# Reordering the last loads of a reading phase: fourth blocks ahead of the streams, raw rows last with no streams between them

## The chip, the cores and the metric

The kernel runs on one core of one Trainium2 chip. The metric is the device time of one execution in microseconds (us), as the median of several runs. In the profile, PE is TensorE (PEld its weight loads), DVE is VectorE, ACT is ScalarE, and SPq is the sequencer that issues the loads and stores.

## The reference

```python
# x: (1, 384, 384, 384) bfloat16, w1d: (1,) bfloat16
g = jnp.einsum("bhwc->bc", x) / (H * W)      # mean of each channel
s = jax.nn.sigmoid(g * w1d[0])               # k = 1, no padding
return x * s[:, None, None, :]
```

Every element must be summed before the first output can be written. x is 113.25 MB and does not fit on the chip, so part of it has to be read a second time.

## The kernel before

A "row" below is one 128 x 384 slab: one position of the arena in each partition, 128 x 384 x 2 = 98,304 bytes. There are 1152. In the **summing phase** each row is loaded and added up by a matmul with ones. Rows end in one of three ways:

- **streams** (785 rows) are summed and then overwritten; the scaling phase reads them again;
- **groups** (296 rows; a "half group" is what one pass of the loop below loads and folds) stay on the chip, packed: a "fold" on VectorE and ScalarE hides the bits of every fourth block in exponent bits of three others that are known to be constant (tested, with a slow way out), so that four rows need the room of three;
- **raw** rows (71) stay as they are, in the space that is free last: 39 rows in three small slots S1, S2, S3, and the scratch areas V, U, Y, T of the folds.

In the **scaling phase** the kept rows are multiplied by the sigmoid and stored, and the streams come through again. The kernel is written as a list of steps with the rows that each reads and writes; waits follow from that list. All loads and stores are issued in order by one sequencer, so a load that must wait for its buffer holds up all loads after it.

```python
S1, S2, S3 = ([slot] for slot in SLOTS)          # 13 rows each
...
BETWEEN = [
    ([], EARLY),                                  # big streams, up to 48 rows a load
    ([], B3), ([], B4),
    ([], B3), ([], AA),
    ([], halves(areas[4])), ([], S1 + S2 + S3),
    (S1, S2, S3 + S1), (S2, S3, S1 + S2 + S3),    # the last two half groups
]
between = sum(n for b in BETWEEN[1:] for where in b for _, n in where)
at = 0
for g, q in enumerate(QS[:BANKED]):
    for lo in range(0, q, 2 * PIECE):
        n = min(2 * PIECE, q - lo)
        *blocks, last = BETWEEN[at]
        cuts = [n * i // len(blocks) for i in range(len(blocks) + 1)]
        for e, f, where in zip(cuts, cuts[1:], blocks):
            group_load(...)                       # three blocks of a piece
            sum_rows(...)
            stream_all(where)
        beside = (U, V)[at % 2]
        group_load(g, 3 * q + lo, 3 * q + lo + n, beside)   # the fourth blocks
        sum_rows(beside, n)
        for k in of_group(g):
            ...                                   # fold(k, ...)
        ...
        stream_all(last)
        at += 1
...
for a, n in SLOTS + [(V, 8), (U, 8), (Y, 8), (T, 5), (T + 5, 3)]:
    take_raw(a, n)                                # load, sum
```

At the end of the summing phase the small slots are thus used in the order S1, S2, S3 as streams, and at once again S1, S2, S3 for raw rows.

## Time and profile before

| | before |
|---|---|
| median of 3 runs | 723.07 us (722.98 to 723.43) |
| span of the profiled run | 721.2 us |
| moved by DMA | 303.87 MB, mean 421 GB/s |
| VectorE busy | 69% of the span |
| TensorE busy | 30% |
| DMA below 360 GB/s | slices 14 and 15 of 40 (252 to 288 us) and the last |

The lines themselves, and how they are read, are in the prediction below. The main dip lies at the turn from the summing to the scaling phase, and the change touches what comes just ahead of it. DMA engines are sixteen, and every load is shared among all of them: the trace has sixteen completion increments for each load.

### The profile page before, as it was taken

How to read it: one execution, taken by the hardware profiler on the slowest of the kernel's cores; microseconds unless marked ns; L12 is line 12 of the kernel's file. 1: busy time of each engine (PE TensorE's matmuls, PEld its weight loads, DVE VectorE, ACT ScalarE, POOL GpSimd, SP SyncE). 2: the span in 40 equal slices, each digit the busy share in tenths (PEclk: the TensorE clock that was granted, in tenths of full speed). 3: DMA queues.
4: the chain of work that ended last, by engine and by line, in shares of the span. 5: the costliest groups of instructions: out<-in, count | busy, mean ns of one | idle time of the engine just before them, and what ended most of it. 6: DMA issues, size and time to landing. Idle time of an engine off the chain costs nothing.

```text
span 721.2 us, 3243 instructions
## 1 busy us (share of the span) xinstructions
PE 213.6 (30%) x1202; PEld 118.9 (16%) x1202; DVE 496.2 (69%) x469; ACT 115.4 (16%) x92; POOL 0.2 (0%) x4
## 2 busy tenths in 40 slices
PE   4677879889877780000000000000000000000000
PEld 2344445545444340000000000000000000000000
DVE  4600006887996729998999998999979994355330
ACT  3600004665774520000100000000000000000000
POOL 0000000000000000000000000000000000000000
PEclk9899999999999995555555555555555555555555
DMA  9999999999999988999999999999999999999997
GB/s 386 426 429 430 444 414 428 432 431 430 427 428 426 418 342 320 408 424 430 432 430 439 424 436 432 427 446 428 428 433 431 441 431 435 422 439 428 438 436 323
DMA packets 19890, 303.87 MB, mean 421 GB/s; under 512 B 2210, under 2 KB 2210, under 8 KB 6434
## 3 DMA queue, kind: packets, MB, share of 16 engines
q1 hardware_dynamic: 19872, 303.67, 98.7%
q8 instruction: 9, 0.15, 0.1%
q14 instruction: 7, 0.06, 0.0%
q10 hardware_dynamic: 2, 0.00, 0.0%
HBM read 190.41 MB, written 113.25 MB: 421 GB/s over the span
## 4 chain that ended last, share of the span: by engine, by line
DMA 56%; DVE 27%; PE 6%; another core or an unknown queue 4%; ACT 2%; SPq 1%; issue 0%; DVEq 0%
DMA arena<-in_x_dram 41%; DVE arena L433 18%; DMA out_dram<-arena 15%; DVE arena L251 6%; PE bank L227 6%; DVE arena L257 4%; ACT arena L291 2%; SPq L221 1%; ACT s_bf L424 0%; PE bank L505 0%; DVE odd L500 0%; DVE odd_i L509 0%; DVE worst L495 0%; DVEq L112 0%
## 5 line engine op out<-in xcount | busy, mean ns | idle before, releaser
L433 DVE TENSOR_TENSOR arena<-arena,s_bf 128x1536 bf16<-128x1536 bf16 (+8 forms) x102 | 241.8, 2411 | 71.8 <-DMA arena<-in_x_dram 57.5
L251 DVE TENSOR_SCALAR arena<-arena 128x1536 uint16<-128x1536 uint16 (+2 forms) x247 | 145.9, 634 | 111.6 <-DMA arena<-in_x_dram 100.8
L227 PE MATMUL bank<-arena,ones 128*128 128x384 bf16 x1152 | 205.4, 340 | 55.0 <-DMA arena<-in_x_dram 54.9
L227 PEld LDWEIGHTS bank<-arena,ones 128*128 128x128 bf16 x1152 | 114.0, 101 | 146.1 <-DMA arena<-in_x_dram 60.7
L257 DVE TENSOR_TENSOR arena<-arena 128x1536 uint16<-128x1536 uint16 (+2 forms) x114 | 121.0, 1062 | 10.3 <-PE bank L227 8.1
L291 ACT ACTIVATE arena<-arena 128x3072 uint16<-128x3072 uint16 (+1 forms) x38 | 102.5, 2696 | 146.1 <-DVE arena L251 146.1
L361 ACT COPY arena<-bank 128x512 uint32<-128x512 uint32 (+1 forms) x7 | 4.0, 571 | 70.5 <-DMA out_dram<-arena 70.3
L242 PE MATMUL bank<-ones,zeros 128*128 128x384 bf16 x48 | 8.3, 326 | 0.0
L291 ACT ACTIVATION_READ_ACCUMULATOR arena<-arena 128x1 f32 x38 | 7.1, 187 | 0.0
L242 PEld LDWEIGHTS bank<-ones,zeros 128*128 128x128 bf16 x48 | 4.7, 98 | 3.1
L505 PE MATMUL bank<-odd,ones 128*128 128x1 bf16 x1 | 0.2, 187 | 15.8 <-DVE odd L500 15.8
L361 ACT COPY bank<-arena 128x512 uint32<-128x512 uint32 (+1 forms) x7 | 3.6, 567 | 0.0
L505 PEld LDWEIGHTS bank<-odd,ones 128*128 128x128 bf16 x1 | 0.1, 106 | 16.2 <-DVE odd L500 16.2
L424 ACT ACTIVATE s_bf<-bank,w_sc 128x384 bf16<-128x384 f32 x1 | 0.6, 581 | 12.9 <-PE bank L227 12.9
L720 ACT ACT_TABLE_LOAD x1 | 1.3, 1283 | 0.7 <-PEq L736 0.7
L321 DVE TENSOR_SCALAR w_sc<-bank 128x1 f32<-128x1 f32 x1 | 0.2, 157 | 1.1 <-PE bank L316 1.1
L311 DVE MEMSET ones<- 128x128 bf16 x1 | 0.2, 165 | 1.0 <-SPq L106 1.0
L316 PE MATMUL bank<-w_bf,ones 1*128 1x1 bf16 x1 | 0.2, 181 | 2.1 <-DMA w_bf<-in_w1d_dram 2.1
L316 PEld LDWEIGHTS bank<-w_bf,ones 1*128 1x128 bf16 x1 | 0.1, 99 | 2.1 <-DMA w_bf<-in_w1d_dram 2.1
L509 DVE CAST odd_i<-bank 128x1 int32<-128x1 f32 x1 | 0.2, 158 | 0.3 <-PE bank L505 0.3
L495 DVE TENSOR_REDUCE worst<-seen 128x1 f32<-128x38 f32 x1 | 0.2, 182 | 0.0
L500 DVE TENSOR_SCALAR odd<-worst 128x1 bf16<-128x1 f32 x1 | 0.2, 156 | 0.0
(5 smaller groups left out, 0.5 us busy)
## 6 DMA issues: line engine op xcount, KB each, us to landing
arena<-in_x_dram SPq DMA_DIRECT2D x17, 4608.0 KB, 34.5
out_dram<-arena SPq DMA_DIRECT2D x6, 4608.0 KB, 43.9
arena<-in_x_dram SPq DMA_DIRECT2D x21, 1248.0 KB, 11.6
arena<-in_x_dram SPq DMA_DIRECT2D x9, 2304.0 KB, 27.3
out_dram<-arena SPq DMA_DIRECT2D x8, 2304.0 KB, 28.1
arena<-in_x_dram SPq DMA_DIRECT2D x4, 4512.0 KB, 33.6
out_dram<-arena SPq DMA_DIRECT2D x3, 4512.0 KB, 26.7
out_dram<-arena SPq DMA_DIRECT2D x9, 1248.0 KB, 12.0
```

What stands on the lines that cost most here:

```text
L221: lambda: nc.sync.dma_start(out=arena[:, a : a + hi - lo, :], in_=view(xf, r0, n)[:, lo:hi, :]),
L227: return nc.tensor.matmul(acc, lhsT=ones[:], rhs=arena[:, i, :], start=first, stop=last)
L242: lambda: nc.tensor.matmul(acc, lhsT=zeros[:], rhs=ones[:, None, :].to_broadcast([P, C // P, P]), start=False, stop=False),
L251: lambda: nc.vector.tensor_scalar(out=dst, in0=src, scalar1=s0, scalar2=s1, op0=op0, op1=op1),
L257: "DVE", lambda: nc.vector.tensor_tensor(out=dst, in0=a, in1=b, op=op), reads=reads, writes=writes
L291: lambda: nc.scalar.activation(out=y, in_=y, func=ACTF.Copy, accum_out=seen[:, 2 * k + i : 2 * k + i + 1]),
L316: lambda: nc.tensor.matmul(votes, lhsT=ones[0:1, :], rhs=w_bf[0:1, 0:1], start=True, stop=True),
L361: "ACT", lambda: nc.scalar.copy(dst.bitcast(u32), src.bitcast(u32)), reads=reads, writes=writes
L424: lambda: nc.scalar.activation(out=s_bf[:], in_=acc, func=ACTF.Sigmoid, scale=w_sc[:, 0:1]),
L433: lambda: nc.vector.tensor_tensor(out=v, in0=v, in1=s_bf[:, None, :].to_broadcast([P, n, C]), op=Op.mult),
L505: lambda: nc.tensor.matmul(votes, lhsT=ones[:], rhs=odd[:], start=True, stop=True),
L720: nc.scalar.preload_act_table(ACTF.Sigmoid)
```

## The change

The intent: load the fourth blocks of the last two half groups before the streams, so that folds can begin sooner and free the scratch areas; move two 13-row streams out of the small slots to the first stream of the kernel; and load the raw rows last, with nothing streamed between them. The diff, cut to its core (comments mine):

```diff
     BETWEEN = [
...
-        (S1, S2, S3 + S1), (S2, S3, S1 + S2 + S3),
+        (S1, S2 + S3 + S1), (S2, S3 + S1),      # two streams of 13 rows fewer
     ]
...
+            blocks = BETWEEN[at]
+            cuts = [lo + n * i // len(blocks) for i in range(len(blocks) + 1)]
             for e, f, where in zip(cuts, cuts[1:], blocks):
...
+                group_load(g, 3 * e, 3 * f, areas[g][0] + 3 * e)
+                sum_rows(areas[g][0] + 3 * e, 3 * (f - e))
+                if e == lo:                      # fourth blocks with the first part
+                    group_load(g, 3 * q + lo, 3 * q + lo + n, beside)
+                    sum_rows(beside, n)
+                for k in of_group(g):
+                    if e <= pieces[k][1] < f:
+                        fold(k, beside + pieces[k][1] - lo)
+                if g:
+                    stream_all(where)
...
-    for a, n in SLOTS + [(V, 8), (U, 8), (Y, 8), (T, 5), (T + 5, 3)]:
+    for a, n in S2 + V1 + S3 + S1 + [(U, 8), (Y, 8), (T, 5), (T + 5, 3)]:
         take_raw(a, n)
```

The first stream becomes 40 rows instead of 14. The scaling phase has the same order of loads and stores in both kernels.

More of the change, by code (lines that the diff above doesn't have):

```diff
@@ L377, in halves @@
         return [(a, n // 2), (a + n // 2, n - n // 2)]
+    V1 = [(V, 8)]
     EARLY = areas[1:5]
     BETWEEN = [
-        ([], EARLY),
-        ([], B3), ([], B4),
-        ([], B3), ([], AA),
-        ([], halves(areas[4])), ([], S1 + S2 + S3),
-        (S1, S2, S3 + S1), (S2, S3, S1 + S2 + S3),
+        (EARLY,),
+        (B3,), (B4,),
+        (B3,), (AA,),
+        (halves(areas[4]),), (S1 + S2 + S3,),
+        (S1, S2 + S3 + S1), (S2, S3 + S1),
     ]
     between = sum(n for b in BETWEEN[1:] for where in b for _, n in where)
+    first = N_STREAM - between
     at = 0
@@ L391 @@
             n = min(2 * PIECE, q - lo)
-            *blocks, last = BETWEEN[at]
-            cuts = [n * i // len(blocks) for i in range(len(blocks) + 1)]
+            beside = (U, V)[at % 2]
+            blocks = BETWEEN[at]
+            cuts = [lo + n * i // len(blocks) for i in range(len(blocks) + 1)]
             for e, f, where in zip(cuts, cuts[1:], blocks):
-                group_load(g, 3 * (lo + e), 3 * (lo + f), areas[g][0] + 3 * (lo + e))
-                sum_rows(areas[g][0] + 3 * (lo + e), 3 * (f - e))
-                stream_all(where)
-            beside = (U, V)[at % 2]
-            group_load(g, 3 * q + lo, 3 * q + lo + n, beside)
-            sum_rows(beside, n)
-            for k in of_group(g):
-                if lo <= pieces[k][1] < lo + n:
-                    fold(k, beside + pieces[k][1] - lo)
-            if g:
-                stream_all(last)
-            else:
-                first = N_STREAM - between
-                stream_all(EARLY[3:], first % 48)
-                stream_all(EARLY, first - first % 48)
-                folding = True
+                group_load(g, 3 * e, 3 * f, areas[g][0] + 3 * e)
[8 more added lines that the diff above has]
+                    stream_all(where)
+                else:
+                    stream_all(EARLY[3:], first % 48)
+                    stream_all(EARLY, first - first % 48)
+                    folding = True
             at += 1
```

## The prediction

> **What bounds the kernel now.** I read the page first: how full the DMA engines are, slice by slice.
>
> ```profile
> span 721.2 us, 3243 instructions
> ...
> DMA  9999999999999988999999999999999999999997
> GB/s 386 426 429 430 444 414 428 432 431 430 427 428 426 418 342 320 408 424 430 432 430 439 424 436 432 427 446 428 428 433 431 441 431 435 422 439 428 438 436 323
> ```
>
> The busiest compute engine, VectorE, is busy for 69% of the span; the DMA row is at nine tenths or more except in two slices. So the kernel is bound by moving 303.87 MB, and only time in which DMA runs below its usual 430 GB/s can be won. Apart from the first and last slices that is the dip of slices 14 and 15 (counting from 0), 252 to 288 us: the end of the summing phase, in which the rows are read and summed, and the start of the scaling phase. Second view: busy times by window around the dip (columns: window, its length, busy time and count of PE, PEld, DVE, ACT, POOL, granted clock, DMA share, GB/s).
>
> ```profile
> 224.00:248.00 24.00, 18.17 (x106) 9.61 (x104) 19.50 (x28) 12.51 (x9) 0.00 (x0) 1.00 1.01 427
> 248.00:256.00 8.00, 4.90 (x29) 2.38 (x26) 7.54 (x11) 5.81 (x5) 0.00 (x0) 1.00 0.99 380
> 256.00:266.00 10.00, 9.61 (x48) 5.07 (x49) 1.55 (x2) 1.67 (x2) 0.00 (x0) 0.83 1.00 417
> 266.00:276.00 10.00, 4.16 (x24) 2.10 (x24) 4.82 (x4) 0.58 (x1) 0.00 (x0) 0.87 0.40 162
> 276.00:286.00 10.00, 0.00 (x0) 0.00 (x0) 10.00 (x6) 0.00 (x0) 0.00 (x0) 0.50 0.97 408
> 286.00:290.00 4.00, 0.19 (x1) 0.11 (x1) 3.65 (x10) 0.00 (x0) 0.00 (x0) 0.50 1.02 286
> ```
>
> In time lost against 427 GB/s: 248 to 256: 8 x 47/427 = 0.9 us; 256 to 266: 0.2; 266 to 276: 6.2; 276 to 286: 0.4; 286 to 290: 1.3. The large one is the turn from reading to writing. The third view, the chain of waits, says what it is made of (start, length, what):
>
> ```profile
> 254.82 2.87 ACT arena L291 x2
> ...
> 257.70 10.02 DMA arena<-in_x_dram
> 267.71 0.05 issue
> 267.76 2.79 PE bank L227 x16
> 270.55 0.02 issue
> 270.57 0.59 ACT s_bf L424
> 271.16 0.02 issue
> 271.18 14.84 DVE arena L433 x8
> ```
>
> Last raw rows, their matmuls, the sigmoid, the first scaling, the first store: nothing can be written before that, and the change keeps all of it. The chain also puts the last folds (two, 243.05 to 257.70 us) in front of that load, as if they held it up. But the load issued at 257.70 landed 10.0 us later because others stood before it in the queue; the loads of the last raw rows landed one behind the other at the queue's pace. So the folds cost nothing now, and the chain misleads here.
>
> That leaves the 0.9 us of 248 to 256. Fourth view: TensorE in time order, with the idle time before each group in brackets.
>
> ```profile
> 246.04 2.29 PE L227 MATMUL bank<-arena,ones 128*128 128x384 bf16 x13 [1.20 <-DMA arena<-in_x_dram]
> 249.08 2.29 PE L227 MATMUL bank<-arena,ones 128*128 128x384 bf16 x13 [0.75 <-DMA arena<-in_x_dram]
> 252.04 2.29 PE L227 MATMUL bank<-arena,ones 128*128 128x384 bf16 x13 [0.68 <-DMA arena<-in_x_dram]
> 256.32 5.91 PE L227 MATMUL bank<-arena,ones 128*128 128x384 bf16 x25 [2.00 <-DMA arena<-in_x_dram]
> ```
>
> Groups of 13 rows start every 3.0 us, then once after 4.28 us. That late group is the first raw slot, S1. Its load was issued at 248.36, the moment the sums of the streamed rows in the same slot ended (246.04 + 2.29 = 248.33): a wait for the buffer. The view of that one issue says how long it took:
>
> ```profile
> DMA to landing us min/median/max: 7.9/7.9/7.9
> ```
>
> The two raw loads behind it also took 7.9 us, the streamed load before it (issued 243.58) 8.4, so 7.9 us is what a 13-row load takes with almost nothing queued ahead.
>
> **What the Trainium skill says.** "DMA: Bandwidth & Descriptors", section "Anatomy of one DMA", gives 2.0 us plus bytes/436e3 (of a DMA issued by GpSimd): for 13 rows of 98,304 bytes, 4.9 us. The trace has 7.9 us here. The same page, "Why a DMA increments its semaphore by 16 and not by 1", explains the rest: a transfer is complete only when all its engines are. The landing records of the late load agree: its first increment comes 4.9 us after the issue, its last 7.9. I use 7.9. "Perfetto Trace Analysis", "Identifying Performance Opportunities", says that repeating bubbles on the saturated engine can mean too few buffers; here it is one bubble, in a chain of three slots. "TensorE: Matmul & The Clock Gate", Part 1, has the clock halve after about 3.4 us of idling; here 2.0 us came before ten matmuls at about 0.32 us instead of 0.176. They did not set the end: TensorE still waited 0.37 us at 267.76.
>
> **The change, part by part.** The scaling phase keeps its order exactly, so I expect it shifted as a block. In the summing phase:
>
> Moved: two 13-row streams (26 rows) leave the small slots near the end; the first stream, into the large area 4, grows from 14 to 40 rows. Bytes are the same, with two loads fewer. From the landing records a 48-row load needs 0.2267 us a row, a 13-row load 0.229: 26 x 0.0023 = 0.06 us won. Everything between comes 26 x 0.2267 = 5.9 us later. At the start, area 4 now waits for 40 rows to be summed instead of 14; but three 48-row loads (33 us) are queued behind them, and TensorE had summed its first 54 rows by 20.7 us, so nothing runs dry.
>
> Removed: the tight reuse of slots. Before, the end is stream S1, S2, S3, then raw S1, S2, S3: from one use of a slot to the next lie 39 rows, 39 x 0.229 = 8.93 us of DMA. One turn needs a landing (7.86 us in the landing records) plus 13 matmuls (2.29) and handover, some 10.2 us. Short by 1.3 us, once, since all three slots then run equally late. That matches the late landing: 4.28 us after its predecessor instead of 2.97, so 1.31. After, the raw order S2, V, S3, S1 with no streams between gives, from the last stream in the slot: S2: S2, 12 group rows, S3, S1 = 51 rows; S3: S3, S1, raw S2, V's 8 = 47 rows; S1: S1, raw S2, V, S3 = 47. 47 x 0.229 = 10.8 us, 0.5 above the need. The kernel before has one reuse at just 47 rows, the load issued at 243.58, which ran without a bubble. So the 1.3 us go, and nothing takes their place. In bandwidth the same is 0.9 + 0.2 = 1.1 us.
>
> Added: nothing. The folds have the same count and operands; loading the fourth block first lets the first of two folds start 25 rows before the last piece has landed. On my estimate the last fold ends at about 255 instead of 257.7 (the last fourth block lands at 240.2, two folds of 7.3 us each follow), and the last raw loads, for Y and T, are due 10 us after that. This takes nothing from the path, but gives margin.
>
> Sum: 1.1 to 1.3 for the bubble, 0.06 for larger loads, perhaps 0.1 for other reuses that grow (from 51 to 59 rows for the first S1 of group 4). I take 1.3: 723.07 - 1.3 = 721.8.
>
> **Rivals.** First: the folds are on the path, as the chain says, and the end of summing moves with them by 257.7 - 255 = 2.7 us: 720.4. For it speaks the chain; against it that the last loads land at the queue's pace. Second: the 47-row turns are still too short, since raw S3 and S1 follow at that distance twice, with margin 0.5 us, and V's load has no slack either: half the gain is lost, 722.5. The 8.4 us of the load at 243.58 speaks against it. Third: the slow packets at 248 to 256 come from memory or from an instruction fetch (the instruction queue has 9 packets in all, one at 252.6) and not from the waiting slot: no change, 723.0. The wait that ends at the very moment of the issue speaks against it. Fourth: a longer start, with the first wait on area 4 breaking the early stream; a loss of some us, and nothing in the queue's depth points to it.
>
> **Range and chances.** The three runs before lie within 0.45 us. All rivals but the last lie within 720.4 to 723.0; I put 8 in 10 on 720.8 to 722.8. 2% is 14.5 us; the whole dip together is worth 9 us, of which about 6 is untouched, so faster by 2% is all but excluded. Slower by 2% would need a new stall of 14 us, for which I see no place.
>
> **What would show it.** Right: no gap before a 13-row group of matmuls above about 1.3 us from 245 to 265 us; GB/s of 248 to 256 at about 425; the slot waits' loads landing in 8.4 us or more; s_bf written about 1.3 us earlier (269.3 instead of 270.57); the span from there on unchanged, near 450.6 us. Wrong: a new gap before the last raw groups, a TensorE chain starting cold in the last 20 us, or a scaling phase whose length changes by more than 0.3 us although its order is the same.

## The result and the profile after

| | before | after |
|---|---|---|
| median, first comparison | 723.03 us (4 runs) | 722.94 us (4 runs) |
| ratio | | 0.9998, 95% interval 0.9981 to 1.0016 |
| span of the profiled run | 721.2 us | 721.1 us |
| sigmoid starts | 270.57 us | 269.79 us |
| from there to the end | 450.58 us | 451.35 us |

Ratios are the mean time of one kernel's fast runs over that of the other's of the same rounds, so not quite the ratio of the quoted medians. The time is the same within the noise. 722.94 lies outside the predicted range of 720.8 to 722.8, and the predicted 1.3 us were not seen.

The page of the changed kernel, rows as in the prediction:

```profile
span 721.1 us, 3241 instructions
...
DMA  9999999999999978999999999999999999999997
GB/s 377 438 432 426 429 433 428 435 431 425 430 422 429 426 329 333 413 426 427 436 429 439 423 431 436 433 439 426 419 432 433 440 437 427 426 435 437 438 428 321
```

The dip is still where it was. Two instructions fewer: the two loads. The windows around it (columns as in the prediction):

```profile
224.00:248.00 24.00, 18.80 (x109) 9.79 (x106) 21.47 (x29) 16.16 (x13) 0.00 (x0) 1.00 1.01 428
248.00:256.00 8.00, 5.00 (x29) 2.68 (x30) 6.12 (x9) 5.39 (x4) 0.00 (x0) 1.00 1.02 428
256.00:266.00 10.00, 8.12 (x50) 4.50 (x49) 0.00 (x0) 0.00 (x0) 0.00 (x0) 1.00 0.98 410
266.00:276.00 10.00, 3.69 (x22) 1.81 (x20) 5.60 (x5) 0.58 (x1) 0.00 (x0) 0.83 0.40 164
```

The lost bandwidth of 248 to 256 us is back, 428 GB/s instead of 380, just as predicted. Yet the window after it is at 410: some engines are done while others are not (the last load's first increment comes at 265.49 us, its last at 268.78). TensorE in time order shows a late group all the same:

```profile
248.67 2.29 PE L227 MATMUL bank<-arena,ones 128*128 128x384 bf16 x13 [0.82 <-DMA arena<-in_x_dram]
251.65 2.29 PE L227 MATMUL bank<-arena,ones 128*128 128x384 bf16 x13 [0.69 <-DMA arena<-in_x_dram]
255.57 3.59 PE L227 MATMUL bank<-arena,ones 128*128 128x384 bf16 x21 [1.64 <-DMA arena<-in_x_dram]
260.36 2.29 PE L227 MATMUL bank<-arena,ones 128*128 128x384 bf16 x13 [1.21 <-DMA arena<-in_x_dram]
```

The third group starts 3.92 us after the second, where 3.0 is the pace. The load it waits for, raw S2, was issued at 245.29 us, 10.2 us before it was complete. Its issue too waited for the slot (the sums of the streamed rows in S2 ended at 245.26), but two 13-row loads stood ahead of it in the queue. The wait left no gap: the first increments of these loads and of raw S2 (246.13, 249.11, 252.07 us) keep the pace. So the late group has another cause. And the chain of waits near the turn:

```profile
253.43 0.97 DVE arena L257
254.40 0.37 SPq L221
...
254.81 12.12 DMA arena<-in_x_dram
...
266.98 2.79 PE bank L227 x16
269.77 0.02 issue
269.79 0.59 ACT s_bf L425
```

The folds end at 254.4 instead of 257.7 us, and the last load then takes 12.1 us instead of 10.0: it stands in a longer queue, as the prediction said of the misleading chain.

So two questions are open. In the summing phase 1.3 us were expected and 0.78 came. In the scaling phase, whose order is the same, even those were lost again.

### The profile page after: what moved, and what is told of

Its sections match the earlier page's. It is cut to its first block, busy times and chain, and to the rows that moved or that the text cites. A ratio compares the mean times of both kernels' runs of the same rounds, so it can differ in the third digit from the quotient of the medians.

```text
span 721.1 us, 3241 instructions
## 1 busy us (share of the span) xinstructions
PE 212.8 (30%) x1202; PEld 118.5 (16%) x1202; DVE 496.3 (69%) x469; ACT 115.4 (16%) x92; POOL 0.2 (0%) x4
## 4 chain that ended last, share of the span: by engine, by line
DMA 52%; DVE 29%; PE 6%; another core or an unknown queue 4%; ACT 3%; SPq 0%; issue 0%; DVEq 0%
DMA arena<-in_x_dram 37%; DVE arena L434 18%; DMA out_dram<-arena 15%; DVE arena L251 7%; PE bank L227 6%; DVE arena L257 4%; ACT arena L291 3%; SPq L221 0%; ACT s_bf L425 0%; PE bank L506 0%; DVE odd L501 0%; DVE odd_i L510 0%; DVE worst L496 0%; DVEq L112 0%
## 6 DMA issues: line engine op xcount, KB each, us to landing
out_dram<-arena SPq DMA_DIRECT2D x9, 1248.0 KB, 12.1
```

## How the landings are read

The trace records each of the sixteen increments of a load's semaphore, one for each DMA engine. For each load there is therefore a first, a mean and a last landing. ("Leading engine" below is the one that lands first, "last engine" the one that lands last. The increments don't name their engines, so from load to load it need not be the same one. The prof views show only the last increment.) For the last load before the turn (3 rows of T) and, as a starting point, the load with 71 rows still to come, in us:

| kernel | last load: first | mean | last | sigmoid starts | last 71 rows took: first engine | mean | last engine |
|---|---|---|---|---|---|---|---|
| before | 267.39 | 267.95 | 269.54 | 270.57 | 18.24 | 17.46 | 17.55 |
| before_again | 267.46 | 267.98 | 269.18 | 270.11 | 18.05 | 17.36 | 17.04 |
| before_third | 266.98 | 267.55 | 269.23 | 270.26 | 17.81 | 17.10 | 17.48 |
| after | 265.49 | 266.83 | 268.78 | 269.79 | 16.38 | 16.46 | 17.18 |
| after_again | 265.44 | 266.80 | 268.87 | 269.88 | 16.38 | 16.46 | 17.10 |
| after_third | 265.55 | 266.74 | 268.62 | 269.63 | 16.38 | 16.46 | 17.30 |
| v_first | 265.60 | 266.90 | 269.21 | 270.24 | 16.37 | 16.46 | 17.58 |
| fourth_first | 267.47 | 268.22 | 269.67 | 270.70 | 17.43 | 17.42 | 17.23 |
| streams_only | 268.96 | 269.28 | 270.00 | 270.96 | 19.73 | 18.93 | 18.63 |
| fewer_sums | 265.64 | 266.89 | 268.38 | 269.40 | 16.38 | 16.37 | 16.38 |
| s1_at_once | 272.62 | 272.84 | 273.06 | 274.04 | 23.23 | 22.38 | 21.18 |
| no_warm | 265.61 | 266.87 | 268.71 | 269.72 | 16.38 | 16.46 | 17.12 |
| y_split | 265.59 | 266.94 | 269.23 | 270.08 | 16.40 | 16.51 | 17.10 |

"First engine" compares the first landings of the two loads, "last engine" their last landings. The rows are explained one by one below. The first six already say the main thing: the change won 1.4 to 1.9 us for the leading engine, 0.6 to 1.0 for the mean, and next to nothing for the last one (17.36 on average before, 17.19 after). The sigmoid waits for the last one.

The slot's wait is also seen in single packets. A starved engine does not show as idle here (the DMA share of 248 to 256 us is 0.99 in before); instead some packets read long. From 244 to 262 us, 20 to 29 packets of 9,984 bytes took 0.49 us or more in the three traces of before, instead of the usual 0.375; in the three of the changed kernel there was one each (0.84 us, near 253 us). The other kernels that let the queue run short of loads for a slot (fourth_first, s1_at_once) have 37 and 22, all the rest none or one. Why these packets read long is not shown.

Theories at this point, as the expectations call them. **A**: the slot's wait was worth 1.3 us and all of it comes through. **B**: the phase ends with the most delayed DMA engine, and the slot's wait held up mostly the leading ones. **C**: the loss in the scaling phase is chance.

## The experiments

The outputs of all eleven runs agreed with the reference. Each was timed against the kernel before on the same chip.

### The changed kernel again, twice, and the kernel before again, twice

No edit.

> The changed kernel once more, unaltered. Theory A (the slot's wait was 1.3 us and all of it comes back at the end, as predicted; the first four runs were unlucky): total 1.0 to 1.3 us below the kernel before, sigmoid near 269.3 us. Theory B (the end of the summing phase is set by the most delayed of the 16 DMA engines; the wait held up mostly the leading ones): sigmoid 0.4 to 0.9 us earlier than the 270.57 of before, mean landing of the last load about 1.1 us earlier, total 0.0 to 0.9 us below. Theory C (the 0.7 us given back in the scaling phase is one chance stall of slow packets near 510 us): no slow packets at 510 us here, and the length from the sigmoid's start to the end back at 450.6 us; if it is systematic, 451.3 us again.

> The kernel before once more, unaltered, for a second trace of its scaling phase. In the first trace it took 450.58 us from the start of the sigmoid to the end; five traces of other kernels with the same scaling order took 451.14 to 451.76. If short stalls come by chance: sigmoid at 570.6 minus 300, that is 270.6 us within 0.2, and 451.1 to 451.8 us from there to the end, with slow packets at other places. If the earlier start itself makes the scaling phase longer (what is won is given back): 450.6 us again.

("570.6 minus 300" is a slip; 270.6 is meant.)

> The changed kernel a third time, beside before_again on the same chip. Sigmoid at 269.8 us within 0.2, so 0.7 to 0.9 us ahead of before_again. Chance stalls: length from there to the end anywhere in 450.6 to 451.8 us, slow packets at places of their own. Systematic giving back: 451.3 us or more, and the total as that of before_again within 0.2.

> The kernel before a third time, for the spread of its summing phase (sigmoid at 270.57 and 270.11 us in two traces). Mean landing of the last load 267.95 within 0.1; its last increment and the sigmoid vary more, 270.0 to 270.7; scaling phase 450.5 to 451.8 us.

| | median us (runs) | kernel before beside it | ratio, 95% interval | sigmoid | sigmoid to end |
|---|---|---|---|---|---|
| after_again | 723.42 (5) | 722.72 (11) | 1.0006, 0.9993 to 1.0019 | 269.88 | 451.76 |
| after_third | 722.44 (5) | 722.94 (9) | 0.9993, 0.9979 to 1.0006 | 269.63 | 450.85 |
| before_again | 723.11 (5) | 722.94 (9) | 0.9999, 0.9986 to 1.0013 | 270.11 | 451.21 |
| before_third | 723.25 (6) | 722.98 (10) | 1.0000, 0.9988 to 1.0013 | 270.26 | 451.92 |

The summing phase repeats well: the sigmoid starts at 269.63 to 269.88 us after, 270.11 to 270.57 before, on average 269.77 and 270.31. The gain there is 0.55 us; the first pair of traces, with 0.78, flattered it. The mean landing is 1.04 us earlier (266.79 against 267.83), so theory A's amount is there, but not at the end of the phase. Several parts of the four texts missed. In after_again the total was 0.7 us above before (by medians), where B had 0.0 to 0.9 below, and the scaling phase took 451.76 us, which is nearer to the "systematic" 451.3 than to 450.6. In before_again the sigmoid came at 270.11, not at 270.6 within 0.2; so after_third was 0.48 us ahead of it, not 0.7 to 0.9. In before_third the mean landing was 267.55, not 267.95 within 0.1.

The scaling phase does not repeat. It took 450.58, 451.21 and 451.92 us before, and 451.35, 451.76 and 450.85 after, the same on average (451.24 and 451.32). The 450.58 of the trace on which the prediction was built is the shortest of all thirteen traces. Part of the difference can be seen in the durations of single packets: nearly all take the time of their size, but in some traces a microsecond or two has many slow ones. Counting, after 290 us, each microsecond in which packets lost over 0.1 us per engine against the median of their size: none in before and after_third, the two shortest of these six; 0.16 us in before_again; 0.34 in after_again (321 and 627 us); 0.63 in after (304, 312 and 510 to 511 us); 0.54 in before_third (322 and 323 us). They differ from trace to trace of one unaltered kernel, and the lengths of the two kernels overlap. That is theory C. But the counted losses do not add up to the lengths (before_again lost 0.16 us and was 0.63 us longer than before), and the places are not just any: counted from the sigmoid's start, over all thirteen traces, most lie near 28, 34, 42 or 51 us. What causes the stalls is not shown.

### v_first: only the raw order, on the kernel before

```diff
-    for a, n in SLOTS + [(V, 8), (U, 8), (Y, 8), (T, 5), (T + 5, 3)]:
+    for a, n in [(V, 8)] + SLOTS + [(U, 8), (Y, 8), (T, 5), (T + 5, 3)]:
```

> The kernel before with one line altered: raw V is loaded before raw S1, S2, S3 instead of after, so 47 rows instead of 39 lie between the uses of each small slot. If the slot's wait is what the change removed, this does as much as the whole change: no gap above 1.3 us before a 13-row group of matmuls, mean landing of the last load about 1.1 us earlier than 267.95. Theory A: total 1.3 us below before. Theory B: sigmoid only 0.4 to 0.9 us earlier, total 0.0 to 0.9 us below. If the order of the folds mattered: nothing gained, sigmoid at 270.6.

Measured: 722.50 us (5 runs), ratio 0.9996 (0.9983 to 1.0009). The leading engine took 16.37 us for the last 71 rows instead of 17.81 to 18.24, the mean landing came at 266.90: with one line, all that the change did to the waiting slot. But the last landing was at 269.21 and the sigmoid at 270.24, inside the range of the kernel before (0.33 us ahead of the 270.57 of its first trace, where B had 0.4 to 0.9). So removing the slot's wait alone did not move the end of the phase, within its own scatter. The text also expected no gap above 1.3 us before a 13-row group; one of 1.49 us came, at 257.8 us. It means nothing: the group follows V's 8 rows, whose matmuls take 1.48 us while the 13-row load takes 2.97. A gap has to be read against the sizes on both sides of it.

### fourth_first: only the fourth blocks first

Streams and raw order as before, in the changed kernel's loop:

```diff
-        (S1, S2 + S3 + S1), (S2, S3 + S1),
+        (S1, S2 + S3 + S1), (S2, S3 + S1 + S2 + S3),
...
-    for a, n in S2 + V1 + S3 + S1 + [(U, 8), (Y, 8), (T, 5), (T + 5, 3)]:
+    for a, n in SLOTS + [(V, 8), (U, 8), (Y, 8), (T, 5), (T + 5, 3)]:
```

> One part of the change alone: fourth blocks first, streams and raw order as before (39 rows between uses of a slot). Slot theories A and B: the gap of 2.0 us before a 13-row group stays, last fold ends 2 to 3 us earlier, sigmoid at 270.6 us within 0.4, total as before within 0.3. Fold theory: sigmoid and total 2 to 3 us earlier.

Measured: 723.69 us (6 runs), ratio 1.0007 (0.9995 to 1.0020), sigmoid at 270.70. The last fold ended at 248.6 us, 9 us earlier than before (I had expected 2 to 3), and nothing was won: the folds were not on the path. (The total, expected within 0.3 us of before, was 0.97 us above it by medians; the interval holds 1.) The mean engine still lost 1.0 us to the slots (17.42 us for the last 71 rows against 16.46). The gap of 2.0 us before a 13-row group, which I had taken for the slot's mark, came out as two smaller ones:

```profile
252.49 2.29 PE L227 MATMUL bank<-arena,ones 128*128 128x384 bf16 x13 [1.36 <-DMA arena<-in_x_dram]
256.26 2.29 PE L227 MATMUL bank<-arena,ones 128*128 128x384 bf16 x13 [1.48 <-DMA arena<-in_x_dram]
```

So a gap on TensorE does not measure the slot's wait: TensorE sees only the last engine.

### streams_only: only the moved streams and the raw order

Fourth blocks last, as before:

```diff
-        (S1, S2, S3 + S1), (S2, S3, S1 + S2 + S3),
+        (S1, S2, S3 + S1), (S2, S3, S1),
...
-    for a, n in SLOTS + [(V, 8), (U, 8), (Y, 8), (T, 5), (T + 5, 3)]:
+    for a, n in S2 + [(V, 8)] + S3 + S1 + [(U, 8), (Y, 8), (T, 5), (T + 5, 3)]:
```

> The other part alone: 26 rows moved to the first stream and the raw order of the changed kernel, but fourth blocks last as before. 60 rows (13.7 us of DMA) then follow the last fourth block, while the two folds take 14.65 us after it lands and the last loads take about 7 us more, against 19.2 us that the queue would need: the folds come onto the path and the sigmoid comes about 4 us later than in the changed kernel, less up to 1 us that lagging engines catch up. Total 2.3 to 3.5 us above before. If folds can't reach the path: 0 to 1 us below before.

Measured: 724.45 us (6 runs), ratio 1.0028 (1.0012 to 1.0043), sigmoid at 270.96. The chain of waits of this kernel:

```profile
260.18 2.87 ACT arena L291 x2
263.04 0.02 issue
263.06 5.04 DMA arena<-in_x_dram
...
268.15 2.79 PE bank L227 x16
270.94 0.02 issue
270.96 0.59 ACT s_bf L424
```

Here the folds are on the path: the load waits for them until 263.06 and then lands in 5.0 us, not 10 or 12, because only one load, issued at 261.11, stands before it. Compare this line with the one of the kernel before: the length of the DMA piece after a wait tells whether the wait cost anything. So the two halves of the change belong together; fourth blocks first is what makes room for fewer streams behind them. The sigmoid came 1.19 us later than in the changed kernel (269.77), not 4: the mean landing is 2.49 us later, the last only 1.24. Engines that lagged caught up while the others waited: the spread of landings fell from 3.46 us to 0.39 at the load issued at 261.11. The total was 1.73 us above before by medians, less than the 2.3 to 3.5 expected.

### s1_at_once: a stall made on purpose

```diff
-    for a, n in S2 + V1 + S3 + S1 + [(U, 8), (Y, 8), (T, 5), (T + 5, 3)]:
+    for a, n in S1 + S2 + V1 + S3 + [(U, 8), (Y, 8), (T, 5), (T + 5, 3)]:
```

> The changed kernel with raw S1 loaded at once after the stream in the same slot: 13 rows between two uses, 10.2 us needed against 2.97 us of DMA, so a stall of 7.2 us by the prediction's working. Theory A (a slot's stall moves the end one for one): sigmoid 7.2 us later than in the changed kernel, 277.0. Theory B (the delayed engines catch up while the leading ones wait): the mean landing of the last load 7 to 8 us later, its last increment only 5.5 to 6.5 us later, the spread of landings below 1.5 us, sigmoid at 275.3 to 276.3; total 5.0 to 6.5 us above the changed kernel's.

Measured: 726.81 us (4 runs), ratio 1.0053 (1.0037 to 1.0068), sigmoid at 274.04. TensorE in time order, and the view of the issue that waited:

```profile
251.93 2.29 PE L227 MATMUL bank<-arena,ones 128*128 128x384 bf16 x13 [0.67 <-DMA arena<-in_x_dram]
259.72 14.28 PE L227 MATMUL bank<-arena,ones 128*128 128x384 bf16 x71 [5.51 <-DMA arena<-in_x_dram]
```

```profile
DMA to landing us min/median/max: 5.4/5.4/5.4
```

This is the decisive number. With really nothing queued a 13-row load takes 5.4 us to its last landing. The prediction had taken 7.9 from the kernel before as the time of an empty queue; there the queue was empty only for the leading engines, and 2.5 of the 7.9 us were the lag of the last one (its backlog, and an instruction fetch near 252.6 us, of which more below). The spread between first and last landing, 2.49 us just before the stall, is 0.46 after it. The sigmoid moved by 4.27 us against the changed kernel, not 7.2: theory A is out. It is also less than the 5.5 to 6.5 that I had written for B; B's direction is right and its amount was still tied to the 7.9. The sum closes with the new number: the last landing of raw S1 came 7.80 us after its predecessor's instead of 2.97, a stall of 4.83 us, and the instruction fetch, at 250.7 us here, left no mark behind the stall (spread 0.44 to the end). It costs the changed kernel 0.8 us (next section). 4.83 - 0.81 = 4.02; the last 71 rows took 21.18 us against 17.19, 3.99 more. The total followed: 3.87 us above the kernel before on the same chip, with the sigmoid 3.73 us above the average of that kernel. A shift of this size reaches the end undiminished.

### fewer_sums: one instruction fetch less

Why do engines lag at all? The instruction queue moves nine packets of 16,384 bytes, each of 0.88 to 0.97 us, during the summing phase, one for about every 128 matmuls (with their 128 weight loads). The last comes at 252.2 us in the changed kernel and 252.6 in the kernel before. This kernel leaves out the matmuls of the first 88 rows, so that the count stays short of the ninth. The sum is wrong; the output still passed the comparison, presumably because the means are close to zero and the sigmoid hardly moves.

```diff
+    SKIP = 88
...
-            first, last = summed[0] == 0, summed[0] == RPP - 1
+            first, last = summed[0] == SKIP, summed[0] == RPP - 1
+            if summed[0] < SKIP:
+                summed[0] += 1
+                continue
```

> Wrong result on purpose: the changed kernel without the matmuls of the first 88 rows (loads, folds and all else unaltered), so that TensorE's instruction stream is 88 of about 128 matmuls shorter than the next instruction fetch needs. Theory B (instruction fetches of 16 KB set one DMA engine back each, and the phase ends with the most delayed one): 8 instruction fetches in the instruction queue instead of 9, none near 252 us; the last increment of the last load comes 2.3 to 2.7 us after the first instead of 3.3 to 3.4; its mean landing near 266.8, its last near 268.0 and the sigmoid near 269.0 us, 0.8 earlier than 269.8. If fetches have nothing to do with it: sigmoid at 269.8 us within 0.2.

Measured: 722.02 us (5 runs), ratio 0.9989 (0.9975 to 1.0003), sigmoid at 269.40. The queue's line of the page, first of the changed kernel and then of this one:

```profile
q8 instruction: 9, 0.15, 0.1%
```

```profile
q8 instruction: 8, 0.13, 0.1%
```

Without the last fetch all engines take the same 16.37 to 16.38 us for the last 71 rows. With it the last engine takes 17.10 to 17.30. So the fetch costs the end of the phase 0.8 us. The sigmoid came only 0.37 earlier, between the two forecasts (0.8, or 0.2 at most), because the last engine happened to lag more before that point (the spread there was 2.75 us, against 2.15 to 2.71 in the three traces of the changed kernel).

### no_warm: the fetch moved

The 48 filler matmuls are in the kernel to keep TensorE's granted clock up. Without them it was 0.663 to 0.672 in the five runs, against 0.670 to 0.679 in those of the changed kernel.

```diff
-    N_WARM = 16
+    N_WARM = 0
```

> The changed kernel without its 48 filler matmuls (three lots of 16 in the first half)[...]. TensorE's instruction stream reaches every later row 48 matmuls earlier in its count, so the last instruction fetch should come 48 rows later, near 263 instead of 252 us. Theory B: the jump of 0.8 to 1.1 us in the last landing moves with it, from the load that lands near 255 us to one that lands after 263 us; sigmoid within 0.4 of the changed kernel's 269.8. If the jump has another cause (the slot, the raw rows): it stays at the load that lands near 255 us. The scaling phase takes 450.6 to 451.8 us by chance.

Measured: 722.63 us (5 runs), ratio 0.9992 (0.9978 to 1.0005), sigmoid at 269.72. The last fetch came at 263.0 us instead of 252.2. The jump of the last landing went with it: the load that lands near 255 us now kept the pace (last landing 254.61, at 0.233 us a row, instead of 255.52 at 0.302), and the one that landed at 265.04 needed 0.333 us a row. The spread of its landings went from 2.35 to 3.17 us. Cause and effect moved together, so the jump belongs to the fetch and not to slot or rows.

### y_split: a try at the tail

```diff
-    ... [(U, 8), (Y, 8), (T, 5), (T + 5, 3)]:
+    ... [(U, 8), (Y, 5), (Y + 5, 3), (T, 5), (T + 5, 3)]:
```

> The changed kernel with the 8 raw rows of Y loaded as 5 and 3. In the changed kernel TensorE sums the last 16 rows in one run of 2.8 us that starts when all 8 rows of Y have landed and ends 1.0 us after the last landing; three rows need 0.55. Expected: sigmoid 0.2 to 0.3 us earlier relative to the last landing (0.7 to 0.8 us after it instead of 1.0). If one load more costs as much as it wins: no change. The total can't show it: chance stalls of the scaling phase are up to 1.2 us.

Measured: 723.25 us (5 runs), ratio 1.0004 (0.9990 to 1.0017). The sigmoid started 0.85 us after the last landing instead of 1.01, so 0.16 us were won there, a little less than expected. The sigmoid itself was at 270.08, since the last engine landed at 269.23 in this trace: a chance lag three times larger than the gain. Inconclusive as an improvement.

No kernel of the series is faster than the kernel before by a margin that the runs can show, and none is offered as better. Two are slower, clear of noise: streams_only and s1_at_once.

## Why the prediction was wrong

- **What bounds the kernel**: right. It is the DMA, the turn's 6 us were untouched, and the scaling phase's order was the same.
- **"So the folds cost nothing now, and the chain misleads here"**: right (fourth_first: folds 9 us earlier, nothing won).
- **The moved streams and the reuses that grow**, 0.06 and perhaps 0.1 us: right in size. Ahead of the last 71 rows the mean landing was 0.20 us earlier (average 250.33 against 250.52).
- **The bubble as lost bandwidth**, 1.1 us: right as a mean over the engines. The last load's mean landing came 1.04 us earlier, 0.85 of it in the last 71 rows and 0.20 ahead of them.
- **"One turn needs a landing (7.86 us in the landing records) plus 13 matmuls (2.29) and handover, some 10.2 us. Short by 1.3 us"**: this step failed. 7.86 is not the time of a load on an empty queue. It holds the backlog of the slowest engine; the empty-queue time is 5.4 us. For the last engine a turn needs 5.4 + 2.3 + 0.05 = 7.8 us, less than the 8.93 that 39 rows give it, so by these numbers it was not short at all. The leading engine's own part lands 4.9 us after the issue (the first increment), but it runs 2.84 us ahead and has to wait for the last one's landing before the slot is summed and free: its turn needs 4.9 + 2.8 + 2.3 + 0.05 = 10.1 us and is short by 1.2. The runs agree: in before, S1's first landings are 10.01 us apart (243.21 and 253.22), 1.1 more than the 8.93. Of the 1.4 to 1.9 us that the change won for the first engine, the 0.3 to 0.8 us beyond this came with the loads behind S1 (raw S2's first landing 3.69 us after S1's in before, instead of 2.97); this working does not cover it. For the last engine 0.16 us was won on average. So the size of the wait was nearly right, but it fell on engines that the phase does not wait for: the overlap was wrong.
- **"That matches the late landing: 4.28 us after its predecessor instead of 2.97, so 1.31"**: a coincidence of size, so the support that it gave was luck. In before_again the same step is 3.48 us, in before_third 4.21. The changed kernel, with no such slot wait, still has one of 3.92. The instruction fetch near 252 us, which costs 0.8 us, comes into the same load in both kernels. The third rival, which named the fetch at 252.6 us and 723.0 us, was dismissed because a wait ended at the very moment of the issue. Both were true in part: there was a wait, mostly of other engines than the last, and it made the slow packets; but the fetch set the last landing back.
- **"I take 1.3"**: of the 1.3 us, 0.55 reach the sigmoid on average: 0.16 in the last 71 rows and 0.40 in the last engine's position before them (251.56 against 251.96), less 0.01 in the steps after the last landing. Of that 0.40, 0.20 is in the mean landing as well; the rest is in the spread of the engines, which varies by as much between traces of one kernel, and may be chance.
- **"I expect it shifted as a block"**: the order was the same, but the length was not. It varies by chance between 450.58 and 451.92 us in the traces, and the kernel before had its shortest in the one trace I used. I also set the range from three runs within 0.45 us; later runs of the same kernel lay between 722.28 and 724.55.

What stays open: whether the 0.55 us arrive in the total. The three ratios 0.9998, 1.0006 and 0.9993 average 0.9999; 0.55 us would be 0.9992. Each interval is about 0.0013 to 0.0018 to either side, so both 0 and 0.55 us are inside. The larger shift of s1_at_once did arrive, which argues for it, but that is an argument and not a measurement of the 0.55. Why the stalls of the scaling phase come is open too. And v_first, fourth_first, streams_only, s1_at_once, fewer_sums, no_warm and y_split have one trace each; differences of the last landing below about 0.5 us between them are within the scatter of one kernel (17.04 to 17.55 us for the last 71 rows in three traces of before).

## What to carry to other kernels

A load that is shared by sixteen engines ends with the last of them, and a short wait for a buffer starves the leading engines first, as here (1.4 to 1.9 us for the first, 0.16 for the last): before counting it as a loss, look at the spread of landings and ask whether the last engine ever ran dry. Take the latency of a load from a queue that is empty for all engines, not from the shortest landing that the trace happens to hold. And before a prediction of a part in a thousand, look at two or three traces of the unchanged kernel: one trace's stage lengths were here uncertain by more than the whole expected gain.

## What the Trainium skill lacked or had wrong

- "Runtime: NRT & Kernel Launch", section "Instruction fetch mechanics", says that instructions are refilled in blocks of 16 KiB, 256 instructions, and that the cost of crossing a block's boundary is "mostly hidden". The block size and the pace agree (16,384 bytes for about 128 matmuls and 128 weight loads). What a fetch takes from data loads the section doesn't say, and in this DMA-bound kernel it was not hidden: in the last 71 rows the last engine needed 17.10 to 17.30 us with a fetch and 16.38 without.
- "DMA: Bandwidth & Descriptors", section "Why a DMA increments its semaphore by 16 and not by 1", says that the engines finish independently, but the page has no figure for how far they drift apart under steady load. Here the spread between first and last landing grew from 1.1 to 1.6 us at the first loads to 2.1 to 2.9 us before the raw rows and lasted until the queue ran dry, when it fell to 0.46 us.
- The same page, section "Anatomy of one DMA", has a fit, for another issuing path, from which 4.9 us for a 13-row load is an estimate. The prediction read 7.9 us in the trace and set the page aside; on a queue empty for all engines s1_at_once has 5.4 us, so the page was nearer than that reading.
- "TensorE: Matmul & The Clock Gate", Part 1, gives about 3.4 us of idling before the clock halves. The trace of before has ten matmuls at about 0.32 us after 2.0 us of idling; in the changed kernel 1.64 us of idling were followed by matmuls at the full rate (21 in 3.59 us).
- None of these pages has the short stalls of packets in the scaling phase: none to 0.63 us in a trace.
